# Zero fill in 10, 8 and 6 pieces, expert 0's W2 after the second gathers, and the last expert's first four tiles between its up passes

## The chip, the cores and the metric

One core of one Trainium2 chip. The metric is the device time of one execution in microseconds (us). A profile of one execution comes with each kernel; its times are us from the start of the span, and its engines are PE (TensorE), DVE (VectorE), ACT (ScalarE), POOL (GpSimd) and SP (SyncE). POOLq and SPq are the instruction queues of POOL and SP.

## The reference

Two layers in a row. First, chunked attention (4 batches, 8 heads, 768 tokens, head size 64): each chunk of 32 queries sees 16 tokens to the left, 8 to the right, and 8 memory tokens. Then a mixture of experts over the 3072 rows of 512 that come out.

```python
for c in range(nc):
    scores = scale * q_c @ concat([mem_k, k_ctx]).T
    out[:, :, c_start:c_end] = softmax(scores) @ concat([mem_v, v_ctx])
x = out.transpose(0, 2, 1, 3).reshape(3072, 512)
noisy_logits = x @ w_gate + log1p(exp(x @ w_noise)) * noise      # 8 experts
top2_w = softmax of the two largest noisy logits of each row
for e in range(8):
    out[mask] += top2_w[mask, k, None] * (relu(x[mask] @ w1[e]) @ w2[e])   # 512 -> 1024 -> 512
```

## The kernel before

**Attention and routing.** A loop runs over 16 pairs of heads, four pairs to a batch. When a batch `b` is finished, its rows stand in the SBUF tile `xrow`. They are written to a DRAM table `x_rows` in two parts by `put_rows`: the 256 words of the row itself, and behind them 8 words with the row's gates. `route(b)` picks the two experts of each row and counts out, expert by expert, a slot for it. Its steps are called by name: `s1`, `s1b` and `s2` make and compare the noisy logits, `s4` writes the gates, `s6` and `s7` add the batch's rows to the table of slots. `decode` turns that table into row numbers: `idx_s` after batch 1, `idx_a` after batch 2, `idx_f` after batch 3.

**Experts.** A slot table has 7 tiles for each expert: 6 of 128 rows and one of 64. Work is cut into ten sets of tiles, in this order: the first four ("sealed") tiles of experts 0 and 1, their last three tiles, and then all seven tiles of experts 2 to 7. For a set, `gather` (L633) fetches the rows of a tile from `x_rows` by an indirect DMA of POOL, `turn` (L656) transposes them on PE, `up` (L685) multiplies by W1 with a relu behind it, and `down` (L701, and L707 for the tile of 64) multiplies by W2. DVE or ACT scales the result by the gates into a tile `ys` (L710, L712), and POOL adds `ys` to the output by an indirect DMA (L713, the scatter). The scatters of the first set write instead of adding. A set's first scatter waits until all scatters of the set before have landed.

**Early start.** Experts 0 and 1 begin before routing is complete. Tiles 0 and 1 of both are gathered with `idx_s` (the first gathers, in `begin_first`), tiles 2 and 3 with `idx_a` (the second gathers), which need the rows and gates of batch 2 in `x_rows`; all others with `idx_f`, which need those of batch 3 too. On PE the order is: up for the first halves of sets 0 and 1, up for their second halves, down of set 0, up of set 2, down of set 1, and so on.

**Order by hand.** The program is scheduled by hand: what stands first in the code goes first into each engine's queue. POOL's queue holds, in this order, the first gathers, the load of W2 of expert 0 (`load_w2`, L585), the write of batch 3's rows, the second gathers, six gathers with `idx_f`, W2 of expert 1, four more gathers, and the first scatters with W1 of expert 2 (`load_w1`, L580) between them. SP's queue holds the zero fill of the output (`zero_fill`, L605) in three parts of 8 pieces (a piece is 128 rows of 2 KB) and the writes of gates (L346) between them. The first part of the fill is started by a small write to the zero tile on DVE (L893), so that it goes out at that place of DVE's queue and not at the start of the kernel.

**The last set.** `up_all` makes the up pass of the four sealed tiles (512 columns), with the turns of the other three between, and then the pass of the last three (320 columns). A `drain` on POOL (L799) and the seven tiles of `down` follow. The end of the kernel waits for the landing of the last scatter. A loop for rows that overflow the slots stands behind it and is not entered with these inputs.

Of the kernel before, what the change touches and what calls it, by code (L numbers as in the profile page):

```python
# [24 lines left out]
def kernel(  # L25
# [63 lines left out]
    def body():  # L89
# [493 lines left out]
        def load_w2(e):  # L583
            w2t = w2p.tile([128, FB, Dm], BF16, name="w2t")
            nc.gpsimd.dma_start(out=w2t, in_=moe_w2[e].rearrange("(fb p) d -> p fb d", p=128))  # L585
            W2[e] = w2t
# [85 lines left out]
        def up(s, c0=0, c1=None):  # L672
            e, tiles = sets[s]
            c1 = total(s) if c1 is None else c1
            if s not in hts:
                small = len(tiles) < NT
                hts[s] = (mp if small else pools["full"]).tile([128, FB, SEALED * CAP if small else SLOTS], BF16, name="hts" if small else "htf", bufs=2)
            k = -(-(c1 - c0) // 512)
            for f in range(FB):
                for c in range(k):  # L680
                    h = hring[cnt["h"] % 3] if hring else tr()
                    cnt["h"] += 1
                    lo, hi = c0 + c * (c1 - c0) // k, c0 + (c + 1) * (c1 - c0) // k
                    for kp in range(KP):
                        nc.tensor.matmul(out=h[:, :hi - lo], lhsT=W1[e][:, kp, f * 128:(f + 1) * 128], rhs=xTs[s][:, kp, lo:hi],  # L685
                                         start=(kp == 0), stop=(kp == KP - 1))
                    relu(hts[s][:, f, lo:hi], h[:, :hi - lo])
                yield "up", s, f

        def down(s, between=()):  # L690
            e, tiles = sets[s]
            ht = hts[s]
            for n, j in enumerate(tiles):
                y = yring[cnt["y"] % 2]
                cnt["y"] += 1
                o, w = (j - tiles[0]) * CAP, width(j)
                gate = gts[s][:, j:j + 1]
                ys = pools["full"].tile([128, Dm], F32, name="ys", bufs=NYS)
                if w == CAP:
                    for f in range(FB):  # L700
                        nc.tensor.matmul(out=y, lhsT=ht[:, f, o:o + w], rhs=W2[e][:, f, :], start=(f == 0), stop=(f == FB - 1))  # L701
                    wide, rows, idx = Dm, out_part[j], (idx_a if s < EARLY else idx_f)[:, e * NT + j:e * NT + j + 1]
                else:
                    wide, rows, idx = Dm // 2, out_part[j].rearrange("n (h d) -> (n h) d", h=2), idx_h[:, e:e + 1]
                    for f in range(FB):
                        for hh in range(2):
                            nc.tensor.matmul(out=y[64 * hh:64 * hh + 64, :wide], lhsT=ht[:, f, o:o + w], rhs=W2[e][:, f, hh * wide:(hh + 1) * wide],  # L707
                                             start=(f == 0), stop=(f == FB - 1))
                if on_act(j % 2):
                    nc.scalar.activation(out=ys[:, :wide], in_=y[:, :wide], func=Act.Copy, scale=gate)  # L710
                else:
                    nc.vector.tensor_scalar(out=ys[:, :wide], in0=y[:, :wide], scalar1=gate, scalar2=None, op0=Alu.mult)  # L712
                ins = nc.gpsimd.indirect_dma_start(  # L713
                    out=rows, out_offset=bass.IndirectOffsetOnAxis(ap=idx, axis=0), in_=ys[:, :wide], in_offset=None,
                    bounds_check=rows.shape[0] - 1, oob_is_err=True, **({"compute_op": Alu.add} if s else {}))

                if n == 0:
                    for old in scat.get(s - 1, ()):
                        tc.add_manual_dep(ins.ins, old.ins.name, mybir.DependencyInfo(mybir.DependencyClass.Sync, mybir.DependencyReason.DATA), reason="rows added to")
                scat.setdefault(s, []).append(ins)  # L720
                if n == 0:
                    for fn in between:
                        fn()
                for _ in range(-(-len(todo) // (len(tiles) - n))):
                    turn(*todo.pop(0))
                yield "down", s, j

        def every():
            half = FIRST * CAP

            def part(s, lo):
                def turns(s):
                    for j in range(lo // CAP, (lo + half) // CAP):
                        if (s, j) in got:
                            turn(s, j)

                turns(s)
                for at in up(s, lo, lo + half):
                    if at[2] == FB - 3 and s + 1 < EARLY:
                        turns(s + 1)  # L740
                    yield at

            for lo in (0, half):
                for s in range(EARLY):
                    yield from part(s, lo)
            def load(fn, e):
                return (lambda: fn(e),) if e < E else ()

            def up_all(s):
                if len(sets[s][1]) < NT:  # L750
                    yield from up(s)
                    return
                late = [(s, j) for j in range(SEALED, NT)]
                for at in up(s, 0, SEALED * CAP):
                    if late and at[2] % 2:
                        turn(*late.pop(0))
                    yield at
                yield from up(s, SEALED * CAP)

            yield from down(0, load(load_w1, EARLY))  # L760
            gather(2 * EARLY, ALL, idx_f, load(load_w2, EARLY))
            todo.extend((EARLY + 1, j) for j in sets[EARLY + 1][1])
            yield from up_all(EARLY)
            yield from down(1)
            gather(2 * EARLY + 1, ALL, idx_f, load(load_w1, EARLY + 1))

            order = [(t, j) for t in range(2 * EARLY + 2, NS) for j in range(NT)]
            runs = {}
            for d, k in zip(range(EARLY, NS - 2), (NT, NT, SEALED, SEALED, SEALED - 1, NT - SEALED)):
                runs[d], order = order[:k], order[k:]  # L770
            assert not order

            def run(d):
                for n, (t, j) in enumerate(runs[d]):
                    gather(t, (j,), idx_f)
                    if n == min(FIRST, len(runs[d]) - 1) and sets[d][0] + 3 < E:
                        load_w2(sets[d][0] + 3)

            for s in range(EARLY + 1, NS):
                e = sets[s][0]  # L780
                while todo and todo[0][0] <= s:
                    turn(*todo.pop(0))
                yield from up_all(s)
                if s < NS - 2:
                    ahead = [(s + 1, j) for j in sets[s + 1][1][:SEALED]]
                    if s < NS - 3:
                        todo.extend(ahead)
                    yield from down(s - 1, load(load_w1, e + 3))
                    run(s - 1)
                if s == NS - 3:  # L790
                    todo.extend(ahead)
                    yield from down(s)
                    run(s)
                if s == NS - 2:
                    todo.extend((s + 1, j) for j in sets[s + 1][1][:SEALED])
                    turn(*todo.pop(0))
                    turn(*todo.pop(0))
                    yield from down(s)
            nc.gpsimd.drain()  # L799
            yield from down(NS - 1)  # L800

        moe = every()

# [10 lines left out]
        def begin_first():  # L814
            decode(tabs[(B - 3) % 2][:, :EARLY * NT], idx_s, None)
            for s in range(EARLY):
                gather(s, range(FIRST), idx_s, upto=(B - 2) * S)
            load_w2(0)

        nc.gpsimd.memset(zt, 0.0)  # L820
        turn_pe(0, 0)
# [66 lines left out]
        warm(2)  # L888
        PV_pe(n - 1)
        exp_act(n)  # L890
        do(r, "s1b", "s2")

        nc.vector.memset(zt[:, :E], 0.0)  # L893
        zero_fill(0, 8)
        PT_pe(n)
        PT_copy(n)
        logits_pe(n - 3)
# [7 lines left out]
        logits_pe(n - 2)  # L905
        xT_pe(n - 1)
        mult_dve(n)
        put_rows(nc.gpsimd, B - 1, 0, XC)
        pctx.close()
        psE = ctx.enter_context(tc.psum_pool(name="psE", bufs=1, reuse_waits="tile"))  # L910
        bankE = [psE.tile([128, 512], F32, name=f"bankE{i}") for i in range(4)]
# [4 lines left out]
        xT_pe(n)  # L916
        do(r, "s4")
        put_rows(nc.sync, B - 2, XC, ROW)
        zero_fill(8, 8)
        do(r, "s5b")  # L920
        logits_pe(n - 1)
        units(1)
# [8 lines left out]
        decode(tabs[(B - 2) % 2][:, :EARLY * NT], idx_a, None)  # L931
        for s in range(EARLY):
            gather(s, range(FIRST, SEALED), idx_a, upto=(B - 1) * S)
        do(last, "s2")
        units(5)
        do(last, "s2b", "s3", "s2c", "s2d", "s4b", "s5", "s5c", "s4")
        put_rows(nc.sync, B - 1, XC, ROW)
        zero_fill(16, 8)
        do(last, "s5b")
        units(6)  # L940
        warm(4)
# [139 lines left out]
```

## Time and profile before

| | us |
|---|---|
| median of 3 runs (lowest, highest) | 331.51 (327.8, 333.48) |
| the profiled execution | 326.7 |
| its span, first to last instruction | 325.0 |

| engine | busy us | share of the span |
|---|---|---|
| PE matmul | 273.6 | 84% |
| POOL | 225.6 | 69% |
| DVE | 160.8 | 49% |
| ACT | 148.3 | 46% |

The span lies 1.7 us under the execution's own time. A share of busy time is a mean over stages: the first 120 us are attention and routing, the rest is the experts. The DMA queue of POOL is q0, that of SP is q1; both are served by the same 16 DMA engines. A row of the timeline gives start, duration, engine, line, operation, and in brackets the engine's idle time before it with what ended it. A row of the chain of waits gives start, duration and what the end of the kernel was then waiting for.

### The profile page before, as it was taken

The page shows a single profiled execution, that of the slowest core. Times are in us where ns is not written, and L with a number is a line of the kernel's source. Part 1 is how long each engine was busy: PE and PEld are TensorE (multiplying, and loading weights), DVE is VectorE, ACT ScalarE, POOL GpSimd, SP SyncE. Part 2 cuts the span into 40 slices and gives each one's busy share as a digit, 9 for nine tenths or more (in the row PEclk, how much of TensorE's full clock was granted, in tenths as well). Part 3 has the DMA queues.
Part 4 walks back from the last instruction along what each step waited for, and adds up shares of the span by engine and source line. Part 5 has one row for each costly group of instructions (what it writes and reads, how often), then busy time and mean ns, then how long its engine had stood idle before and what let it go on. Part 6 is the DMA issues. An engine that isn't in the chain of part 4 may idle for free.

```text
span 325.0 us, 7669 instructions
## 1 busy us (share of the span) xinstructions
PE 273.6 (84%) x3077; PEld 173.6 (53%) x3097; DVE 160.8 (49%) x367; ACT 148.3 (46%) x293; POOL 225.6 (69%) x219
## 2 busy tenths in 40 slices
PE   2878768787849719999999999999999999999940
PEld 1666656666638518565555465465454555555420
DVE  6478689889995823332344342342342434324210
ACT  6868878788656514224343423423422224234110
POOL 8997788667422178665888777887886888584480
PEclk9989989797998958999999999999999999999995
DMA  9999999999999996999999999999999979788393
GB/s 105 167 153 180 174 172 185 206 162 226 222 233 304 361 372 130 216 230 193 143 209 157 246 177 215 205 184 191 201 209 216 172 128 182 156 109 116 39 131 46
DMA packets 99847, 60.30 MB, mean 186 GB/s; under 512 B 65056, under 2 KB 84768, under 8 KB 99808
## 3 DMA queue, kind: packets, MB, share of 16 engines
q0 software_dynamic: 82160, 50.63, 107.0%
q1 hardware_dynamic: 14272, 8.98, 9.4%
q10 hardware_dynamic: 3376, 0.16, 1.0%
q8 instruction: 26, 0.43, 0.5%
q14 instruction: 13, 0.11, 0.1%
HBM read 65.07 MB, written 23.27 MB: 272 GB/s over the span
## 4 chain that ended last, share of the span: by engine, by line
PE 60%; DMA 10%; POOL 8%; issue 7%; DVE 7%; ACT 3%; POOLq 1%; DVEq 0%
PE bankE L701 22%; PE bankE L685 15%; PE bankT L685 8%; POOL out_dram L713 4%; PE bankT L656 4%; DMA x_rows<-xrow 3%; DMA xl<-x_rows,idx_s 3%; PE bankE L707 2%; DMA xl<-x_rows,idx_a 2%; DMA qg<-in_q_dram 2%; PE bankO L331 2%; PE bankT L257 2%; PE bankO L328 2%; POOL vp L134 1%; DVE mx L298 1%
## 5 line engine op out<-in xcount | busy, mean ns | idle before, releaser
L713 POOL DMA_INDIRECT out_dram<-ys,idx_f x40 | 62.9, 1574 | 24.1 <-DVE ys L712 12.7
L685 PEld LDWEIGHTS <-w1t 128*128 128x128 bf16 x576 | 55.3, 99 | 34.2 <-issue 3.9
L701 PE MATMUL bankE<-w2t,htf 128*128 128x512 bf16 x278 | 64.7, 379 | 0.5
L633 POOL DMA_INDIRECT xl<-x_rows,idx_f x48 | 50.0, 1042 | 16.2 <-issue 9.1
L712 DVE TENSOR_SCALAR ys<-bankE,gt 128x512 f32<-128x512 f32 (+1 forms) x32 | 21.9, 684 | 62.6 <-PE bankE L701 49.5
L685 PE MATMUL bankE<-xTf,w1t 128*128 128x320 bf16 (+1 forms) x250 | 51.3, 338 | 1.7 <-ACT xTf L658 1.3
L710 ACT ACTIVATE ys<-bankE,gt 128x512 f32<-128x512 f32 x24 | 16.5, 687 | 67.7 <-PE bankE L701 54.9
L701 PEld LDWEIGHTS <-htf 128*128 128x128 bf16 x288 | 27.4, 98 | 29.8 <-issue 0.2
L134 POOL DMA_DIRECT2D vp<-in_v_dram x34 | 33.6, 992 | 10.8 <-PE bankT L316 3.9
L670 DVE TENSOR_SCALAR htf<-bankE 128x512 bf16<-128x512 f32 (+1 forms) x32 | 18.9, 591 | 28.4 <-PE bankE L685 28.4
L668 ACT ACTIVATE htf<-bankE 128x512 bf16<-128x512 f32 (+1 forms) x32 | 16.5, 517 | 27.5 <-PE bankE L685 26.7
L685 PE MATMUL bankT<-xTf,w1t 128*128 128x320 bf16 (+1 forms) x128 | 27.8, 339 | 0.3 <-DVE htf L670 0.3
L267 ACT COPY kT<-bankT 64x768 bf16<-64x768 bf16 x32 | 25.3, 790 | 5.4 <-PE bankT L257 4.9
L656 PE MATMUL bankT<-identb,xl 128*128 128x128 bf16 (+1 forms) x224 | 20.7, 220 | 7.8 <-DMA xl<-x_rows,idx_a 5.7
L656 PEld LDWEIGHTS <-xl 128*128 128x128 bf16 (+1 forms) x224 | 15.5, 99 | 21.0 <-DMA xl<-x_rows,idx_a 6.7
L701 PE MATMUL bankE<-w2t,hts 128*128 128x512 bf16 x92 | 22.2, 379 | 0.2
L685 PE MATMUL bankE<-xTs,w1t 128*128 128x256 bf16 (+1 forms) x128 | 19.3, 291 | 0.7 <-ACT xTs L658 0.7
L298 DVE TENSOR_REDUCE mx<-bankS 128x12 f32<-128x768 f32 x16 | 15.2, 953 | 8.1 <-PE bankS L293 8.1
L257 PE MATMUL bankT<-identb,qg 128*64 128x128 bf16 x192 | 10.2, 253 | 10.2 <-DMA qg<-in_q_dram 8.1
L670 DVE TENSOR_SCALAR htf<-bankT 128x512 bf16<-128x512 f32 (+1 forms) x16 | 9.5, 591 | 15.6 <-PE bankT L685 14.4
L309 ACT ACTIVATE P<-sd 128x768 bf16<-128x768 f32 x16 | 13.5, 844 | 6.0 <-DVE sd L304 5.9
L713 POOL DMA_INDIRECT out_dram<-ys,idx_a x8 | 10.4, 1297 | 8.2 <-issue 4.2
(188 smaller groups left out, 451.3 us busy)
## 6 DMA issues: line engine op xcount, KB each, us to landing
w1t<-in_moe_w_dram POOLq DMA_DIRECT2D x8, 1024.0 KB, 12.3
w2t<-in_moe_w_dram POOLq DMA_DIRECT2D x8, 1024.0 KB, 10.7
out_dram<-zt SPq DMA_DIRECT2D x3, 2048.0 KB, 17.8
vp<-in_v_dram POOLq DMA_DIRECT2D x30, 168.0 KB, 8.2
qg<-in_q_dram POOLq DMA_DIRECT2D x16, 192.0 KB, 7.1
kg<-in_k_dram POOLq DMA_DIRECT2D x16, 192.0 KB, 7.4
x_rows<-xrow SPq DMA_DIRECT2D x2, 792.0 KB, 10.3
x_rows<-xrow SPq DMA_DIRECT2D x1, 768.0 KB, 8.5
```

What stands on the lines that cost most here:

```text
L134: nc.gpsimd.dma_start(out=vp[p0 + j:p0 + j + nj, c:c + m, hh, :], in_=bass.AP(v.tensor, v.offset + (hd * S + c * chunk + j - left_ctx) * D ...
L257: nc.tensor.transpose(out=p_t[64 * hh:64 * hh + 64, j, :], in_=src[:, hh, j * D:(j + 1) * D], identity=identb)
L267: nc.scalar.copy(kbufs[n % 2][hs, hh].rearrange("d (p j) -> d p j", j=SJ), p_t[hs])
L298: nc.vector.tensor_reduce(out=mx, in_=st[n]["ps"], axis=AX, op=Alu.max)
L633: nc.gpsimd.indirect_dma_start(out=xl, out_offset=None, in_=xd[:upto], in_offset=bass.IndirectOffsetOnAxis(ap=idx[:, c:c + 1], axis=0), bo ...
L656: nc.tensor.transpose(out=p_t[:, kp, :w], in_=xl[:w, kp * 64:(kp + 1) * 64].bitcast(BF16), identity=identb[:w, :w])
L668: nc.scalar.activation(out=dst, in_=src, func=Act.Relu)
L670: nc.vector.tensor_scalar(out=dst, in0=src, scalar1=0.0, scalar2=None, op0=Alu.max)
L685: nc.tensor.matmul(out=h[:, :hi - lo], lhsT=W1[e][:, kp, f * 128:(f + 1) * 128], rhs=xTs[s][:, kp, lo:hi], start=(kp == 0), stop=(kp == KP ...
L701: nc.tensor.matmul(out=y, lhsT=ht[:, f, o:o + w], rhs=W2[e][:, f, :], start=(f == 0), stop=(f == FB - 1))
L712: nc.vector.tensor_scalar(out=ys[:, :wide], in0=y[:, :wide], scalar1=gate, scalar2=None, op0=Alu.mult)
L713: ins = nc.gpsimd.indirect_dma_start(out=rows, out_offset=bass.IndirectOffsetOnAxis(ap=idx, axis=0), in_=ys[:, :wide], in_offset=None, bou ...
```

## The change

Five edits:

- The first part of the zero fill goes out ahead of routing steps `s1b` and `s2` of batch 2 on DVE, not behind them, and has 10 pieces. The second and third parts have 8 and 6.
- The write of batch 3's rows (768 KB) moves from POOL's queue to SP's, behind the gates of batch 2 and ahead of the second part of the fill.
- W2 of expert 0 is loaded behind the second gathers and no longer behind the first.
- In the last set, the down tiles 0 to 3 and their scatters stand between the two up passes, with the `drain` ahead of them; tiles 4 to 6 stay at the end.
- `down` gets an argument `of`, the tiles that it makes; the wait for the scatters of the set before is tied to the set's first tile.

```diff
-        def down(s, between=()):
+        def down(s, between=(), of=None):
...
-            for n, j in enumerate(tiles):
+            of = of or tiles
+            for n, j in enumerate(of):
...
-                if n == 0:
+                if j == tiles[0]:
                     for old in scat.get(s - 1, ()):
...
-            def up_all(s):
+            def up_all(s, middle=()):
...
                     yield at
+                yield from middle
                 yield from up(s, SEALED * CAP)
+
+            def sealed_down(s):
+                nc.gpsimd.drain()
+                yield from down(s, of=sets[s][1][:SEALED])
...
-                yield from up_all(s)
+                yield from up_all(s, sealed_down(s) if s == NS - 1 else ())
...
-            nc.gpsimd.drain()
-            yield from down(NS - 1)
+            yield from down(NS - 1, of=sets[NS - 1][1][SEALED:])
...
                 gather(s, range(FIRST), idx_s, upto=(B - 2) * S)
-            load_w2(0)
...
         exp_act(n)
+
+        nc.vector.memset(zt[:, :E], 0.0)
+        zero_fill(0, 10)
         do(r, "s1b", "s2")
-
-        nc.vector.memset(zt[:, :E], 0.0)
-        zero_fill(0, 8)
...
         mult_dve(n)
-        put_rows(nc.gpsimd, B - 1, 0, XC)
...
         put_rows(nc.sync, B - 2, XC, ROW)
-        zero_fill(8, 8)
+        put_rows(nc.sync, B - 1, 0, XC)
+        zero_fill(10, 8)
...
             gather(s, range(FIRST, SEALED), idx_a, upto=(B - 1) * S)
+        load_w2(0)
...
         put_rows(nc.sync, B - 1, XC, ROW)
-        zero_fill(16, 8)
+        zero_fill(18, 6)
```

More of the change, by code (lines that the diff above doesn't have):

```diff
@@ L723, in down @@
                         fn()
-                for _ in range(-(-len(todo) // (len(tiles) - n))):
+                for _ in range(-(-len(todo) // (len(of) - n))):
                     turn(*todo.pop(0))
```

## The prediction

> **What bounds the kernel now.** I read the page first, then the chain of waits from 80 to 125 us, PE's waits from 119 us on, POOL's timeline, and the chain at the end.
>
> ```profile
> span 325.0 us, 7669 instructions
> w2t<-in_moe_w_dram POOLq DMA_DIRECT2D x8, 1024.0 KB, 10.7
> out_dram<-zt SPq DMA_DIRECT2D x3, 2048.0 KB, 17.8
> ```
>
> The last two rows are DMA issues with the median time to landing: a W2 load takes 10.7 us, one part of the zero fill 17.8.
>
> ```profile
> 87.20 9.95 DMA xl<-x_rows,idx_s
> 97.20 0.61 PE bankT L656 x4
> ...
> 101.38 10.11 DMA x_rows<-xrow
> ...
> 112.30 0.33 POOL xl L633
> ...
> 113.88 6.64 DMA xl<-x_rows,idx_a
> 120.57 0.62 PE bankT L656 x4
> ```
>
> This is the chain where the stages meet. From 101.38 to 111.49 the kernel waits for 24 KB of batch 2's gates; they stand on SP's queue behind 2 MB of zeros. Only then can POOL issue the second gathers (112.30), and PE waits for these until 119.69.
>
> ```profile
> PE bankT L656 <- DMA xl<-x_rows,idx_a: 5.7, 2, 5.4
> PE bankE L685 <- ACT xTf L658: 1.3, 2, 0.7
> PE bankE L685 <- ACT xTs L658: 0.7, 1, 0.7
> PE bankT L685 <- DVE htf L670: 0.3, 1, 0.3
> ```
>
> From 119 us to the end PE waited for nothing but this: after the gathers 2.3 us in all. By this view alone PE is the bound, and every us that it starts earlier would be won. POOL's timeline says otherwise:
>
> ```profile
> 112.30 1.27 POOL L633 DMA_INDIRECT xl<-x_rows,idx_a  x1 [10.17 <-DVE xrow L438]
> ...
> 117.86 1.01 POOL L633 DMA_INDIRECT xl<-x_rows,idx_f  x1 [0.30 <-issue]
> ...
> 125.44 0.96 POOL L585 DMA_DIRECT2D w2t<-in_moe_w_dram  x1
> 126.70 1.09 POOL L633 DMA_INDIRECT xl<-x_rows,idx_f  x1 [0.30 <-issue]
> ...
> 133.39 1.04 POOL L713 DMA_INDIRECT out_dram<-ys,idx_a  x1 [1.65 <-DVE ys L712]
> ...
> 139.33 0.98 POOL L713 DMA_INDIRECT out_dram<-ys,idx_a  x1 [1.03 <-ACT ys L710]
> ...
> 148.97 1.63 POOL L713 DMA_INDIRECT out_dram<-ys,idx_a  x1 [3.63 <-issue]
> ...
> 283.91 1.62 POOL L713 DMA_INDIRECT out_dram<-ys,idx_f  x1 [2.70 <-DVE ys L712]
> ```
>
> Only the first set's scatters (133.39 to 139.33) start when their ys is done. The second set's first one goes at 148.97 and waits for the landing of the one issued at 139.33. The next view has the landing times of such scatters and, for a late set, the ys that its first scatter carries:
>
> ```profile
> out_dram<-ys,idx_a POOLq DMA_INDIRECT x5, 8.3
> ...
> 278.69 0.75 DVE L712 TENSOR_SCALAR ys<-bankE,gt 128x512 f32<-128x512 f32 x1 [1.35 <-PE bankE L701]
> ```
>
> 139.33 + 8.3 = 147.6, so the landing explains 148.97. At 283.91 the ys had been ready since 279.44, 4.5 us earlier, though the row names DVE as the last releaser: again the set before has to land. So from 133 us on two chains run side by side, PE with its matmuls, and POOL with scatters, gathers, loads and landings, and POOL's is the later one until the last set:
>
> ```profile
> 296.71 6.05 issue
> 302.76 0.03 POOLq L713
> ...
> 303.11 0.75 DVE L712 TENSOR_SCALAR ys<-bankE,gt 128x512 f32<-128x512 f32 x1 [1.24 <-PE bankE L701]
> 304.13 1.55 POOL L713 DMA_INDIRECT out_dram<-ys,idx_f  x1 [7.42 <-DVE ys L712]
> ...
> 315.28 1.55 POOL L713 DMA_INDIRECT out_dram<-ys,idx_h  x1 [0.30 <-issue]
> ```
>
> POOL's last scatter of the set before ends at 296.71, its queue goes on at 302.76 (the drain stands between), and PE's first ys is ready at 303.86. The two chains arrive 1 us apart, and seven scatters follow, (315.28 - 304.13)/6 = 1.86 us apart.
>
> **The change part by part.**
>
> *First part of the fill.*
>
> ```profile
> 91.77 0.20 DVE L386 TENSOR_TENSOR nl<-ns,nz_all 128x48 f32<-128x48 f32 x1
> ...
> 93.41 0.07 DVE L893 MEMSET zt<- 128x8 f32 x1
> 93.54 0.38 SPq L605 DMA_DIRECT2D out_dram<-zt  x1
> ...
> q1 hardware_dynamic: 379, 0.78, 56.8%
> q0 software_dynamic: 373, 0.38, 55.8%
> ...
> 112.00:117.00 5.00, 1.06 (x13) 0.89 (x13) 2.75 (x10) 0.00 (x0) 3.79 (x4) 0.70 1.07 376
> ```
>
> The small write goes ahead of s1b, which begins at 91.77: the fill is issued 93.41 - 91.77 = 1.6 us earlier. The two q rows are the DMA queues from 98 to 102 us, with packets and MB: SP's and POOL's share the engines packet for packet, and the fill moves at 0.78/4 = 195 GB/s. What stands in POOL's queue there is W2 of expert 0, and later the write of batch 3's rows. Both leave that queue. The last row (112 to 117 us, 376 GB/s at its end) is nearly the fill alone. So 10 pieces (2.62 MB) take 2.62/0.376 = 7.0 us instead of 2.1 MB in most of 17.8. With the first packets some 3.5 us after the issue, they are through by about 103 us and the gates of batch 2, written at 101.38, land by 105, not at 111.49. The two added pieces cost 0.52/0.376 = 1.4 us of that. The price is the first gathers, which land at 97.2 and now share engines with the fill for up to 97.2 - 95.5 = 1.7 us; packet for packet that is between 0 and 1.7 us. I take **+0.5**, since few of their packets are then left. It shifts all that follows on DVE.
>
> *Second gathers, PE.* They now wait for their row numbers:
>
> ```profile
> 105.74 0.17 DVE L570 TENSOR_TENSOR idx_a<-row,emp 128x14 int32<-128x14 f32 x1
> ...
> 115.55 0.22 DVE L570 TENSOR_TENSOR idx_f<-row,emp 128x56 int32<-128x56 f32 x1
> ...
> 112.64 0.90 PE L480 MATMUL bankT<-col,Rn 128*128 128x56 f16 x12 [1.20 <-DVE Rn L468]
> ```
>
> So they go at about 106.4 instead of 112.30. With 6.6 to 7.4 us to the turn, as before, PE can turn at about 113.9, just after the routing matmuls that end at 113.54, not at 119.69. PE leads by 5.8 us and avoids most of the slow clock after its wait (about 1 more).
>
> *W2 of expert 0.* POOL issues it behind four second gathers, 106.4 + 5.2 = 111.6. It shares engines with the second and third fill parts. Packet for packet with the rest of the third part I get the landing near 125 us; bounds are 111.6 + 10.7 = 122.3 (the page's median) and 111.6 + 17.8 = 129.4 (if it goes at the fill's pace). PE wants it for the down of set 0, at 130.86 before and about 124 now, so PE's lead shrinks to some 5 us. By the Trainium skill (DMA: Bandwidth & Descriptors, "Measured"), a lone 1 MB load is busy for 6.15 us; an estimate from that page would be a landing at 118 and no wait. No row here shows a weight load that fast; the sum would stay the same.
>
> *POOL's chain.* The gathers with idx_f wait for that table, 115.77 + 0.5, so they start at 116.3 instead of 117.86: **-1.5** us. The gates and rows of batch 3 must have landed too: SP now carries 2.62 + 0.79 + 2.1 = 5.5 MB ahead of these gates, at 300 to 376 GB/s from 95.5 on, 110 to 114. Six gathers, W2 of expert 1 and four gathers follow in 133.39 - 1.35 - 117.86 = 14.2 us (1.65 us of idle time, of which 0.3 stays), and then the first scatter, whose ys is ready (PE leads): 130.5, **-2.85**. One new wait: in this program POOL's DMAs take eight semaphores in turn, and the first gather behind W2 of expert 1 is the eighth DMA behind W2 of expert 0. It needs that landing (125) when it is due at 126.70 - 1.5 = 125.2; I add **+0.45**, between 0 and 129.4 - 125.2 = 4.2, near the end that my landing is nearest to. Queued behind it are three gathers and all scatters. So the chain is **-2.4** us. From 133 us on the rest of it is scatters, loads and landings that move as one, and I carry -2.4 to the drain. DMA agrees with a gain of that size and no more:
>
> ```profile
> 122.00:127.00 5.00, 5.00 (x41) 4.07 (x40) 1.60 (x4) 1.97 (x7) 4.09 (x5) 0.78 0.48 139
> ```
>
> From 122 to 127 us the DMA engines are half idle (0.48), some 2.6 us, and that gap is where W2 goes.
>
> *Last set.* PE does the same work in another order, and its relus are done before the down that needs them. The seven scatters now wait for POOL alone: 302.76 + 0.37 of queue + 0.26 = 303.4 instead of 304.13, **-0.75**. The last three can follow at 1.86 us: their ys come at or before. If PE had been late, the change would save here; with a lead of 5 us PE would have been early anyway. Bounds: 0 (1.86 us apart is POOL's own pace) and 302.76 - 304.13 = -1.4.
>
> **Sum:** -2.4 - 0.75 = **-3.15** us. Against the profiled execution 326.7 - 3.2 = 323.5; that execution lies 4.8 under the median, so for the runs I say 331.51 - 3.2 = **328.3**.
>
> **The rivals.**
>
> 1. *PE's lead goes through* (the gaps in POOL's chain are slack that shrinks). For it: PE's waits above. Gain 5.2 + 0.75 = 6, up to 5.8 + 1 + 0.75 = 7.6 if W2 is no wait: 323.9 to 325.5. Against it: scatters that start 4.5 us after their ys and wait for landings.
> 2. *W2 of expert 0 comes too late* (the other side). If its 1024 KB go at the shared 0.38/4 = 95 GB/s from 111.6 + 5 on, they need 11 us and land at 127.7, with slower engines 129.4. The gather that waits for its semaphore then goes at 129.4 instead of 126.70, the first scatter at 129.4 + 5.34 = 134.7 instead of 133.39, +1.35, less 0.75: +0.6, 332.1. It decides from a landing at 128 on.
> 3. *The larger fill keeps its old pace.* 17.8 x 1.25 = 22.2 us from 92 on: gates at 114, second gathers at 114.8, W2 issued at 120, landing at 130.7 by 10.7. The first scatter goes at 136.0, +2.6, and with loads pushed behind it up to +6: 334 to 337. Against it: what shared the engines with the fill is gone.
> 4. *Nothing moves*: the gates land early, but the gathers with idx_f do not, because batch 3's gates land at 118 behind more on SP's queue: -0.75 alone, 330.8.
>
> **How the numbers follow.** Forecast 0.46, rival 1 0.19, rival 2 0.13, rival 3 0.12, rival 4 0.10. 2% (6.6 us) is about what a measurement of this kernel can tell from no change; its own runs spread over 5.7 us. Faster by more than that is rival 1's upper half and a little of the forecast: 0.16. Slower is the upper end of rival 3 and loads pushed back in rival 2: 0.12. The range takes in rival 1 up to 7.6 us with 1 us of the runs' spread, and rivals 2 and 4 and the lower half of 3: 322.5 to 334.5.
>
> **What would show it.** Right: the second gathers issued near 106.4, PE turning at 114, the first fill landing some 7 us earlier; the gathers with idx_f near 116.3; the first scatter near 130.9, the second set's first one near 146.5, lags between ys and scatter 2 to 3 us larger than before, the sealed scatters right behind the drain at 300.3 to 301, the last one near 312.1. Wrong: the first scatter after 133.4, a PE wait for W2 of expert 0 beyond 2 us, or a drain that ends over 5 us earlier (rival 1).

## The result, and the profile after

The changed kernel takes 325.56 us (median of 20 runs, 323.05 to 328.23) where the kernel before takes 329.47 (20 runs, 325.81 to 333.48). The ratio is 0.9929, 95% interval 0.9903 to 0.9955: 0.7% faster, which is the same at the bound of 2%. Forecast was 328.3 us and a gain of 3.15 us; the medians differ by 3.9, the ratio is worth 2.3 us. Ratios leave out runs over 1.5% longer than the shortest of their kernel, which leaves only three or four runs in e7, e8, e9 and e12 below, so these have the medians of all runs beside them. The profiled execution took 325.68 us, against 326.7 before, so the two profiles differ by only 1.0 us; the section on the prediction comes back to that.

In these profiles the scatter's line is L714 and that of ys L711 or L713 (one or two lines further down in e7 to e11). Span and DMA issues of the changed kernel's page, as in the first fences of the prediction:

```profile
span 324.0 us, 7669 instructions
out_dram<-zt SPq DMA_DIRECT2D x1, 2560.0 KB, 9.6
```

The first part of the fill is now 2.5 MB and lands in 9.6 us, where a part of 2 MB took 17.8. Its issue and POOL's timeline:

```profile
94.53 0.38 SPq L605 DMA_DIRECT2D out_dram<-zt  x1
...
106.63 1.12 POOL L633 DMA_INDIRECT xl<-x_rows,idx_a  x1 [4.99 <-DVE idx_a L570]
...
112.34 0.99 POOL L585 DMA_DIRECT2D w2t<-in_moe_w_dram  x1
118.87 1.09 POOL L633 DMA_INDIRECT xl<-x_rows,idx_f  x1 [5.54 <-DVE hts L670]
...
126.54 0.96 POOL L585 DMA_DIRECT2D w2t<-in_moe_w_dram  x1
127.90 1.09 POOL L633 DMA_INDIRECT xl<-x_rows,idx_f  x1 [0.40 <-PE bankE L685]
...
133.26 1.04 POOL L714 DMA_INDIRECT out_dram<-ys,idx_a  x1 [0.30 <-issue]
...
148.52 1.63 POOL L714 DMA_INDIRECT out_dram<-ys,idx_a  x1 [3.27 <-DMA out_dram<-ys,idx_a]
...
284.00 1.62 POOL L714 DMA_INDIRECT out_dram<-ys,idx_f  x1 [2.69 <-DMA out_dram<-ys,idx_h]
...
303.93 1.55 POOL L714 DMA_INDIRECT out_dram<-ys,idx_f  x1 [7.11 <-DVE htf L670]
...
315.08 1.55 POOL L714 DMA_INDIRECT out_dram<-ys,idx_h  x1 [0.30 <-issue]
```

Set these beside the rows of before. The fill did not go out earlier in this execution (94.53, before 93.54): it landed early chiefly because W2 has left POOL's queue, as e3 shows below; what batch 3's rows add to that was not tested apart. The second gathers go at 106.63 and no longer at 112.30. But the gathers with `idx_f` start at 118.87, one us *later* than before (117.86), the first scatter at 133.26 (133.39), and the last at 315.08 (315.28). POOL's chain has not moved. PE's has:

```profile
114.72 0.71 PE L656 MATMUL bankT<-identb,xl 128*128 128x128 bf16 x8
...
277.21 0.75 DVE L713 TENSOR_SCALAR ys<-bankE,gt 128x512 f32<-128x512 f32 x1 [1.35 <-PE bankE L702]
```

PE turns the second gathers at 114.72 and not at 119.69. The ys of the scatter at 284.00 is ready at 277.96, 6.0 us ahead of it; before, it was 4.5 us ahead of the one at 283.91. So PE got a lead, and it stands in POOL's queue. But it is not the 5.0 us of the turn: the first ys on DVE is done at 129.85 and not at 133.11, 3.3 us earlier, and the one at 277.96 is 1.5 us earlier than its counterpart before (279.44). The gap in DMA between 122 and 127 us (0.48 busy before) is closed (windows: PE, PEld, DVE, ACT and POOL busy, granted clock, DMA share, GB/s):

```profile
122.00:127.00 5.00, 3.00 (x22) 1.82 (x19) 0.85 (x2) 0.90 (x3) 4.09 (x5) 1.00 1.06 265
```

Why did the start of POOL's chain not move? The row at 118.87 names DVE as its releaser, but the table was ready earlier:

```profile
115.86 0.22 DVE L570 TENSOR_TENSOR idx_f<-row,emp 128x56 int32<-128x56 f32 x1
```

It ends at 116.08, 0.2 us ahead of the forecast's 116.27 (115.77 + 0.5). The gathers wait another 2.8 us for the gates of batch 3, which SP issued at 112.31:

```profile
112.31 0.36 SPq L346 DMA_DIRECT2D x_rows<-xrow  x1
112.72 0.54 SPq L605 DMA_DIRECT2D out_dram<-zt  x1
```

In the trace the semaphore of a write is counted up in 16 steps. For this write 15 of them come between 114.48 and 116.14, the last at 118.09, and the gathers start 0.78 us behind it. The 0.78 us return in e3, e4 and e8 (119.55 and 120.33; 121.83 and 122.61; 118.49 and 119.27), so the gates' landing is what ended the wait. The fill ahead of the gates has a late step too (the trace has four of its 16, three at 111.79 to 111.83 and one at 114.62), which suggests that one share of the gates stood behind a share of the fill; that is not shown.

### The profile page after: what moved, and what is told of

The parts are those of the page before. It is cut to its first block, busy times and chain, and to the rows that moved or that the text cites. A ratio compares the mean times of both kernels' runs of the same rounds, so it can differ in the third digit from the quotient of the medians.

```text
span 324.0 us, 7669 instructions
## 1 busy us (share of the span) xinstructions
PE 276.9 (85%) x3077; PEld 175.0 (54%) x3097; DVE 161.6 (50%) x367; ACT 148.4 (46%) x293; POOL 225.4 (70%) x218
## 5 line engine op out<-in xcount | busy, mean ns | idle before, releaser
L714 POOL DMA_INDIRECT out_dram<-ys,idx_f x40 | 63.0, 1575 | 23.6 <-issue 8.2
L685 PEld LDWEIGHTS <-w1t 128*128 128x128 bf16 x576 | 54.5, 98 | 38.4 <-issue 7.3
L713 DVE TENSOR_SCALAR ys<-bankE,gt 128x512 f32<-128x512 f32 (+1 forms) x32 | 21.9, 684 | 61.4 <-PE bankE L702 41.4
L711 ACT ACTIVATE ys<-bankE,gt 128x512 f32<-128x512 f32 x24 | 16.5, 688 | 68.8 <-PE bankE L702 45.1
L670 DVE TENSOR_SCALAR htf<-bankE 128x512 bf16<-128x512 f32 (+1 forms) x32 | 18.9, 592 | 28.5 <-PE bankE L685 21.4
L656 PE MATMUL bankT<-identb,xl 128*128 128x128 bf16 (+1 forms) x224 | 20.0, 215 | 0.4 <-ACT xt L356 0.4
L343 DVE TENSOR_TENSOR xrow<-bankO,rec 128x768 bf16<-128x768 f32 x16 | 15.3, 958 | 0.9 <-DMA x_rows<-xrow 0.4
```

The costliest lines, as they stand in the source:

```text
L656: nc.tensor.transpose(out=p_t[:, kp, :w], in_=xl[:w, kp * 64:(kp + 1) * 64].bitcast(BF16), identity=identb[:w, :w])
L670: nc.vector.tensor_scalar(out=dst, in0=src, scalar1=0.0, scalar2=None, op0=Alu.max)
L714: ins = nc.gpsimd.indirect_dma_start(out=rows, out_offset=bass.IndirectOffsetOnAxis(ap=idx, axis=0), in_=ys[:, :wide], in_offset=None, bou ...
```

## Experiments

The table puts the kernels together; each number is the start of an instruction in that kernel's profile. "Gate wait" is POOL's idle time in front of the gather behind W2 of expert 1; 0.30 is no wait. "Set 9 last" is the last scatter of the last but one set. Medians and ratios are those of the runs, against the kernel before on the same chip. A profiled execution of this table can lie up to 1.8 us from its kernel's median (e1: 326.94 and 325.14), so two rows tell of 1 or 2 us only where the waits in them say so.

| kernel | `idx_f` gathers | gate wait | first scatter | set 9 last | last scatter | median us | ratio (95%) |
|---|---|---|---|---|---|---|---|
| before | 117.86 | 0.30 | 133.39 | 295.16 | 315.28 | 327.8 to 329.5 | 1 |
| after | 118.87 | 0.40 | 133.26 | 295.26 | 315.08 | 325.56 | 0.9929 (0.9903 to 0.9955) |
| e1 start only | 116.87 | 1.89 | 132.71 | 293.83 | 316.96 | 325.14 | 0.9925 (0.9895 to 0.9955) |
| e2 last set only | 117.53 | 0.30 | 134.59 | 294.13 | 315.52 | 327.12 | 0.9981 (0.995 to 1.0012) |
| e3 W2 early | 120.33 | 0.30 | 134.52 | 295.72 | 316.40 | 326.37 | 0.9948 (0.9911 to 0.9985) |
| e4 gates on ACT | 122.61 | 0.30 | 136.89 | 300.12 | 320.15 | 328.70 | 1.0006 (0.9967 to 1.0046) |
| e5 fill 10, 4, 10 | 117.18 | 4.56 | 135.71 | 297.06 | 316.32 | 326.91 | 0.9958 (0.9923 to 0.9993) |
| e6 no second fill | 115.68 | 2.44 | 132.10 | 293.63 | 312.90 | 323.33 | 0.9866 (0.9809 to 0.9923) |
| e10 e5 and gov early | 116.44 | 5.23 | 135.63 | 296.80 | 316.00 | 326.00 | 0.9938 (0.9913 to 0.9963) |
| e12 after again | 117.55 | 2.37 | 133.88 | 296.37 | 315.89 | 325.53 | 0.9841 (0.9796 to 0.9886), by medians 0.993 |

### The two halves of the change: e1 and e2

e1 is the changed kernel with the last set as before; e2 is the kernel before with the last set's new order.

```diff
 e1:
-yield from up_all(s, sealed_down(s) if s == NS - 1 else ())
+yield from up_all(s)
...
+nc.gpsimd.drain()
-yield from down(NS - 1, of=sets[NS - 1][1][SEALED:])
+yield from down(NS - 1)
```

> The changed kernel with its last set as before: seven down tiles behind both up passes. Theory (two chains that arrive together at the last set, POOL's and PE's; the edits at the start give PE a lead of 3 us or more that POOL's chain doesn't have): PE's ys of the last set wait for the drain and no longer the other way round, so the ratio is 0.991 to 0.997, about that of the whole change, the first scatter of the last set stands right behind the drain, and the lag between ys and scatter in the sets before is 2 to 3 us larger than before. Rival (PE is the bound): PE's lead goes through, ratio 0.985 to 0.990, lags as before. Rival (all of the gain is at the last set): ratio 0.998 to 1.002.

> The kernel before with nothing but the last set's order changed: tiles 0 to 3 of its down between the two up passes. Theory (two chains): PE is taken out of the tie at the end by 7 us, the seven scatters stand right behind the drain, ratio 0.992 to 0.998; not additive with the edits at the start, which do the same to PE by another way. Rival (PE is the bound): PE's order changes and its sum does not, ratio 0.998 to 1.002. Lags in the sets before the last: as before in both.

Measured: e1 0.9925, e2 0.9981. What can be measured comes from the start; the interval of e2 takes in no change and reaches into both of its forecasts. In e1's profile the first scatter of the last set waits for PE, not for the drain as expected. PE had been held up at 253 us by a load named `gov`, which the section on e9 explains:

```profile
253.56 0.36 DVE L977 TENSOR_TENSOR gov<-gov,miss 128x192 f32<-128x192 f32 x1 [3.46 <-DMA gov<-x_rows]
...
305.81 1.55 POOL L714 DMA_INDIRECT out_dram<-ys,idx_f  x1 [10.44 <-DVE ys L713]
```

PE lost 2.7 us there, and the granted clock was 0.79 from 254 to 262 us, where it was 1.00 in the changed kernel's profile. So in one execution PE can lose its lead and be the later chain at the end (10.44 us of idle time, where 7.11 stood after the drain in the changed kernel). The medians of e1 and of the changed kernel are alike.

In e2's profile the first scatter of the last set goes 1.25 us earlier than before (302.88), but the fifth waits for PE, whose second up pass now stands in front of it:

```profile
311.81 1.55 POOL L714 DMA_INDIRECT out_dram<-ys,idx_f  x1 [1.80 <-DVE ys L713]
```

So the new order alone gives nothing at the last scatter (315.52, before 315.28). The changed kernel has no wait there, but its fifth ys is ready at 308.80 for a scatter at 311.36: 2.6 us ahead, not the 6 us of the first.

### W2 of expert 0 early again: e3

```diff
 gather(s, range(FIRST), idx_s, upto=(B - 2) * S)
+load_w2(0)
...
 gather(s, range(FIRST, SEALED), idx_a, upto=(B - 1) * S)
-load_w2(0)
```

> The changed kernel with W2 of expert 0 loaded behind the first gathers again. Theory: the first part of the fill shares the engines with it again, the gates of batch 2 land 2 to 4 us later than in the changed kernel and the second gathers with them; PE's lead shrinks by as much and is not missed at the end; POOL's chain starts when batch 3's gates are there and has no wait for W2 of expert 0 (the first gather behind W2 of expert 1). Ratio to before 0.990 to 0.999, within 1.5 us of the changed kernel. Rival (PE is the bound): 2 to 4 us slower than the changed kernel.

Measured: 0.9948. The second gathers go at 111.92 again, as the fill shares the engines with W2, and the `idx_f` gathers at 120.33, as batch 3's gates land later (119.55). The gate wait is 0.30, because W2 has long landed. The first scatter is at 134.52. The second gathers are 5.3 us later than in the changed kernel, where 2 to 4 were expected. Loading W2 later is what gives the second gathers their 5 us, and about 1.3 us at the first scatter in these profiles.

### Batch 3's gates on a queue of their own: e4

```diff
-put_rows(nc.sync, B - 1, XC, ROW)
+put_rows(nc.scalar, B - 1, XC, ROW)
```

> The changed kernel with batch 3's gates written from ACT's queue, not from SP's behind the second part of the fill. Theory (POOL's chain decides, and it starts when batch 3's gates have landed, 118.1 us in the changed kernel): the gathers with the last table start when their row numbers are ready, 116.4 instead of 118.9, the first scatter goes 0.7 to 2.5 us earlier (the lower end if the landing of W2 of expert 0 then holds the chain) and the end with it: ratio 0.984 to 0.991. Rival (PE is the bound, or another wait takes over at once): the same as the changed kernel, 0.992 to 0.994.

Measured: 1.0006, the other way. From the page's DMA part of 100 to 125 us, and POOL's timeline:

```profile
x_rows<-xrow ACTq DMA_DIRECT2D x1, 24.0 KB, 8.8
...
122.61 1.09 POOL L633 DMA_INDIRECT xl<-x_rows,idx_f  x1 [8.51 <-DVE hts L670]
...
136.89 1.04 POOL L714 DMA_INDIRECT out_dram<-ys,idx_a  x1 [0.30 <-DVE ys L713]
```

24 KB took 8.8 us to land, and the gathers waited 8.51 us. The edit does more than was meant: SP no longer stops for these gates, so it issues the third part of the fill right behind the second, at 104 us and not at 112.72. From 113 to 116 us SP's queue moved 440 packets, of the fill, and ACT's none; ACT's first packets move between 116.5 and 117 us, as the fill runs out, and 673 of its 784 from 117 to 118. By the Trainium skill (DMA: Bandwidth & Descriptors, "Queues, rings and completion order") an engine goes round its queues packet by packet; this trace does not show that for ACT's queue and SP's, and why ACT's packets started so late is not shown. The last step of the gates' semaphore came at 121.83. What the run does show: with the start of POOL's chain 3.6 us later (136.89 to 133.26), the last scatter is 5.1 us later and the whole gain is gone, though PE's work is the same.

### No second fill part: e6

```diff
-zero_fill(10, 8)
```

> The changed kernel with the second part of the zero fill (8 pieces, 2 MB) left out, so that those rows of the output are not cleared; nothing else differs. It makes the two conditions of the forecast true that failed: batch 3's gates have no fill ahead of them and should land by 113 instead of 118.1, and W2 of expert 0 should land near 122 to 124 instead of 127. Theory (the start of POOL's chain sets the end): the gathers with idx_f at 116.4 instead of 118.87, no idle time before the gather behind W2 of expert 1, first scatter at 130.5 to 131 instead of 133.26, second set's first one near 146, and every scatter down to the last one about 2.3 us earlier; ratio to the kernel before 0.986. Rival (PE's chain sets the end since the change): PE starts no earlier than in the changed kernel, so the last scatter stays at 315 and the ratio at 0.993.

Measured: 0.9866. The `idx_f` gathers at 115.68 are those of the forecast (116.3), as the table is then all that they wait for. But the gather behind W2 of expert 1 waited:

```profile
123.34 0.96 POOL L585 DMA_DIRECT2D w2t<-in_moe_w_dram  x1
126.75 1.09 POOL L633 DMA_INDIRECT xl<-x_rows,idx_f  x1 [2.44 <-ACT gt L645]
```

The releaser shown is not the cause. In the trace this gather waits for the semaphore that W2 of expert 0 holds. Where the landing of W2 is on record, the gather goes 0.8 us behind it: 126.6 and 127.37 in e1, 127.7 and 128.54 in e12, 129.6 and 130.36 in e5. In e2 and e3, where W2 is loaded early, it waits 0.30 us. Here W2 lands near 126. That is the forecast's new wait, 2.1 us beyond the usual 0.30, where it put 0.45. The first scatter at 132.10 is 1.2 us earlier than in the changed kernel, not 2.3, and the last, at 312.90, 2.2 us: the ratio came as forecast, but half of the gain arose behind the start. PE is 1.9 us earlier here too (first ys of the last set at 296.14 and not at 297.99), which the rival had left out. What speaks against PE setting the end is that this ys lay ready for 5.6 us before its scatter at 301.75.

### The fill in 10, 4 and 10 pieces: e5

```diff
-zero_fill(10, 8)
+zero_fill(10, 4)
...
-zero_fill(18, 6)
+zero_fill(14, 10)
```

> The changed kernel with the zero fill cut as 10, 4 and 10 pieces instead of 10, 8 and 6: half of the second part goes behind batch 3's gates. Theory (the start of POOL's chain sets the end, and it has two gates, the landing of batch 3's gates and that of W2 of expert 0): the gates land near 115.5 instead of 118.1, so the gathers with idx_f start near 116.8 instead of 118.87, but as much fill as before still shares the engines with W2, which lands at 127 to 128, and the gather behind W2 of expert 1 waits for it; first scatter 132.5 to 133.3 instead of 133.26, time 0 to 0.7 us shorter than the changed kernel, ratio to the kernel before 0.991 to 0.993. Rival (the gates alone set the start): the whole 2 us, first scatter at 131.2, ratio 0.987.

Measured: 0.9958. The gates are no wait now (117.18, 3.0 us behind W2's issue, as the table is ready), but W2 is:

```profile
130.36 1.09 POOL L633 DMA_INDIRECT xl<-x_rows,idx_f  x1 [4.56 <-ACT gt L645]
...
PE bankE L702 <- DMA w2t<-in_moe_w_dram: 3.1, 1, 3.1
```

The two gates are as expected; the size was not. W2 took 16.4 us and landed at 129.6, not at 127 to 128, and PE waited for it too (3.1 us). What the gates gained W2 lost, and the first scatter was 2.4 us later. Two rows of the changed kernel's DMA from 118 to 122 us show the price (queue, packets, MB, share of the 16 engines):

```profile
q0 software_dynamic: 370, 0.38, 58.0%
q1 hardware_dynamic: 351, 0.71, 52.6%
```

W2's packets write 1 KB and the fill's 2 KB, their numbers are nearly equal, and each takes its engine about as long: 4 us x 16 x 0.58/370 = 100 ns, and 96 ns. So, counted in the profile's packet time, 1 MB of W2 costs the engines what 2 MB of fill cost, and beside the fill it moves at 95 GB/s.

### Less work on PE, less on POOL: e7, e8, e9, e11

e7 leaves out half of the second matmul of the seventh set, e8 four of its seven scatters, e9 both.

```diff
 e7:
+nf = FB // 2 if s == EARLY + 4 else FB
-for f in range(FB):
+for f in range(nf):
...
 e8:
+if s != EARLY + 4 or n < 2 or n == len(of) - 1:
-ins = nc.gpsimd.indirect_dma_start(
+    ins = nc.gpsimd.indirect_dma_start(
...
```

> The changed kernel with half of the second matmul left out in one set (24 matmuls of 512 columns of the seventh set, six tiles), so the rows of that set are wrong; scatters, loads and landings are all kept. PE has 5 us less to do from 239 us on. Theory (POOL's chain sets the end, PE is 3 to 6 us early): the lags between ys and scatter grow by about 5 us from that set on and the last scatter stays near 315: ratio to the kernel before 0.993, the changed kernel's own. Rival (PE sets the end): 5 us shorter, ratio 0.978.

Measured: median 326.39 against 325.56 of the changed kernel (ratio 0.9867, interval 0.9788 to 0.9947, by medians 0.992; too wide to tell the two theories apart). The profiled execution, of 326.42 us, does tell: the first ys of the last set, and its first and last scatter.

```profile
293.51 0.75 DVE L714 TENSOR_SCALAR ys<-bankE,gt 128x512 f32<-128x512 f32 x1 [1.26 <-PE bankE L703]
...
305.16 1.55 POOL L715 DMA_INDIRECT out_dram<-ys,idx_f  x1 [6.65 <-issue]
...
316.30 1.55 POOL L715 DMA_INDIRECT out_dram<-ys,idx_h  x1 [0.31 <-issue]
```

In the changed kernel this ys was ready at 297.99, 5.9 us ahead of its scatter; here at 294.26, 10.9 us ahead. Five us of PE's work were taken away, and in this execution all of them went into waiting for POOL.

> The changed kernel with four of the seven scatters of the seventh set left out (third to sixth tile), so those rows lack that expert; all matmuls are kept. POOL's chain is 4 x 1.86 = 7.4 us shorter at 253 us. Theory of two chains with PE's lead small at the end: the next set's first scatter at 257.0 instead of 264.4, then PE becomes the later chain (ys of the last but one set ready at 278.0, last ys at 311.3), so the last scatter goes near 311.6 instead of 315.1: 3.5 us shorter, ratio 0.982, and waits for ys are back in front of the last scatters. Rival 1 (PE sets the end already): no change, 0.993. Rival 2 (POOL alone, PE far ahead): the whole 7.4 us, 0.970.

Measured: 0.9822, interval 0.9756 to 0.9888, and a median of 323.39 (by medians 0.983): the number that two chains gave (0.982), between the two rivals. The profiled executions of e8 and e9 took 328.02 and 327.38 us, well above the medians, so waits are read from them and no times. In e8's the waits for ys are back, as expected:

```profile
303.76 1.55 POOL L715 DMA_INDIRECT out_dram<-ys,idx_f  x1 [7.15 <-DVE ys L713]
...
314.56 1.55 POOL L715 DMA_INDIRECT out_dram<-ys,idx_f  x1 [3.67 <-DVE ys L713]
```

But PE is 5 us later in that execution than in the changed kernel's (first ys of the last set at 303.25 and not at 297.99), so these rows alone do not show what the missing scatters did.

> The changed kernel with both cuts together: half of the second matmul of the seventh set and four of its seven scatters left out. Theory of two chains: PE is 5 us earlier and POOL 7.4 us, so the sum is bound by POOL again with PE 1 to 4 us ahead: 6.5 to 7.4 us shorter than the changed kernel, ratio near 0.972, more than the two single cuts together (0 and 3.5). If the two cuts simply add, PE's cut would have had to show alone.

Measured: 0.9806 (0.9732 to 0.988), median 323.75 (by medians 0.984). This missed: it should have been 0.972. PE's waits and DVE's row say what came between:

```profile
PE bankE L703 <- DVE ys L714: 7.0, 1, 7.0
...
255.29 0.36 DVE L978 TENSOR_TENSOR gov<-gov,miss 128x192 f32<-128x192 f32 x1 [7.72 <-DMA gov<-x_rows]
```

`gov` is a load of all gates for the loop on overflowing rows, 96 KB in packets of 32 bytes on ACT's queue. Its first use stands in DVE's queue ahead of a ys, and PE cannot go on before that ys. In e8 PE lost 2.6 us to it, and in the changed kernel the same load holds DVE for 1.05 us:

```profile
gov<-x_rows ACTq DMA_DIRECT2D x1, 96.0 KB, 27.1
...
252.08 0.36 DVE L976 TENSOR_TENSOR gov<-gov,miss 128x192 f32<-128x192 f32 x1 [1.05 <-DMA gov<-x_rows]
```

So PE's lead can end here: DVE was ready for `gov` at 247.57 in e9 and had it at 255.29, 29 us after its issue. It is not so each time: in e7 `gov` was used at 248.06 without a wait, 21.4 us after its issue, so PE's 5 us could pass. e11 is e9 with this load issued earlier:

```diff
-until("down", NS - 5, NT - 1)
+until("down", 3, NT - 1)
 gov = lp.tile([128, NP, E], F32, name="gov")
 nc.scalar.dma_start(out=gov, ...)
```

> The two cuts together (half of the second matmul of the seventh set and four of its seven scatters left out) with the gov load issued some 50 us earlier. With the two cuts alone PE waited 7.0 us for a ys that stood on DVE behind gov's landing, and that ate what the cuts should have given. Theory: with that wait gone PE is 5 us earlier, POOL 7.4 us, POOL is the later chain and the last scatter goes 6.5 to 7.4 us earlier than in the changed kernel, near 308: ratio to the kernel before 0.970 to 0.975. Rival (something else held the two cuts back): ratio stays near 0.981 with a wait somewhere else.

Measured: 0.9649 (0.9618 to 0.968), median 316.24 and the last scatter at 307.97 (forecast near 308): 9.3 us under the changed kernel, of which 7.1 show in the profile. The ratio lies below the forecast's 0.970 to 0.975; where the rest comes from is not shown. The load took as long as ever (28.1 us), but nothing waits for it. The first scatter of the last set waits for nothing but the drain, the fifth waits 1.2 us for a ys:

```profile
295.62 1.55 POOL L716 DMA_INDIRECT out_dram<-ys,idx_f  x1 [6.55 <-issue]
...
304.25 1.55 POOL L716 DMA_INDIRECT out_dram<-ys,idx_f  x1 [1.51 <-DVE ys L714]
...
307.97 1.55 POOL L716 DMA_INDIRECT out_dram<-ys,idx_h  x1 [0.30 <-issue]
```

So work pays where it is taken from both chains, once the third one (`gov`) is out of the way: the intervals of e9 and e11 do not meet. From PE alone it paid nothing in the profile, from POOL alone 2.2 us by medians and 3.5 by ratios. No run has the early `gov` with one cut only, so what each cut is worth without that wait is not shown.

### A version that might be better: e10, beside e12

e10 has the fill of e5 and the early `gov`; e12 is the changed kernel itself, on the same chip.

> The fill as 10, 4 and 10 pieces, and the load of the gates for the overflow (gov, 3072 packets of 32 bytes on ACT's queue) issued behind the fourth set's down instead of the sixth's, so some 50 us earlier. In the changed kernel it took 27 us to land and its first use stands on DVE in front of a ys. Theory (POOL sets the end, PE leads): the wait of DVE for gov goes (1.1 us in the changed kernel's profile, 3.5 to 7.7 in some of the others), PE's lead grows by that, and the time is at most 0.7 us shorter than the fill order alone makes it, since only executions in which PE was the later chain gain. Rival (PE's waits set the end): 1 to 3 us shorter.

> The changed kernel as it is, on the same chip as the fill order and the gov load, to compare them with: ratio to the kernel before 0.993.

Measured: e10 0.9938, median 326.00; e12 median 325.53, which is 0.993 of the 327.81 before, as expected. In e10 no wait of PE for ys is left, but W2 of expert 0 holds POOL for 5.23 us and PE for 2.9. Beside e5 (326.91) the early `gov` is worth 0.9 us, between the two forecasts and within the runs' spread. No version here beats the changed kernel.

## Why the prediction was right, and where it was not

**The chains.** The main reading held: PE's waits make PE look like the bound, but its lead is lost in POOL's queue. PE was to turn at 113.9 and turned at 114.72. The lags between ys and scatter were to grow by 2 to 3 us and grew by 1.5 (4.5 to 6.0), since only 1.5 us of PE's 5.0 are left at 278 us. In e7's profile 5 us less of PE give no us at the end. Rival 1 falls with that, as far as one execution tells.

**The fill.** The second gathers were forecast for 106.4 and went at 106.63. Rival 3 falls: 2.5 MB landed in 9.6 us. The part of the reason that failed is the issue 1.6 us earlier: it came 1.0 us later. The price on DVE, +0.5, held in this profile (the table of the second gathers is ready at 106.37, before at 105.91), but it is 1.0 to 2.3 us in e1, e7, e9, e11 and e12; e2, with the old start, has 0.7, so part of it is the spread between executions.

**The start of POOL's chain, -1.5.** This step failed in the profile: +1.0. The table was in time, but the gates of batch 3 were taken to land between 110 and 114 and landed at 118.09. The forecast divided bytes by a rate. That misses when SP can issue (112.31, behind the routing) and the one late share. The time is that of rival 4, but its reason, more fill ahead on SP's queue, holds for one late share at most: that queue had all but run empty (10 packets from 112 to 113 us), and 15 of 16 shares had landed by 116.14. In e1, e7, e9, e11 and e12, which have the same order of transfers there, SP issued the gates at 112.9 to 114.2 and they had landed by 116.0 to 117.0, before the table. There the gathers went at 116.87 to 118.21, because the table itself was later: 1.0 us earlier than before at best, and 0.4 later at worst.

**The eight-semaphore wait, +0.45.** The mechanism was right and the size was wrong. Where the gates were in time, the wait was 1.6 to 4.9 us beyond the usual 0.30 (1.89 in e1, 2.37 in e12, 4.56 in e5, 5.23 in e10). W2 was taken to land at 125; it landed near 126 even with 2 MB less of fill (e6). In the changed kernel's profile the late gates hide it (0.40): POOL's chain has two gates that feed on the same DMA engines, and bytes moved from one to the other (e5) only change which is last. So -2.4 became -0.1 in that profile, and in all seven profiles with this order of transfers the first scatter goes between 132.71 and 134.38, where 130.9 was forecast. (The working also says that the sum would stay the same if W2 landed at 118 without a wait; by its own terms it would be -3.6.)

**The last set, -0.75.** POOL's chain reaches the last set 0.1 us later than before (295.26 and 295.16), and its first scatter goes 0.2 us earlier (303.93 and 304.13), so the term measured -0.3: the wait behind the set before shrank from 7.42 to 7.11 us, and 6.55 is seen where nothing else is late (e11). In e2 the runs cannot tell it from nothing, and the prediction's "the last three can follow at 1.86 us" failed there: the fifth scatter waited for PE.

**The sum.** The two profiles give -1.0 us (326.7 to 325.68), of which the last scatter's start has 0.2 and what comes behind it 0.8. The runs give -2.3 by the ratio. The range held and the number was near, but not by the path that was worked out, so the nearness is luck: the two terms that made it up, -2.4 and -0.75, measured -0.1 and -0.3. The signs set down for POOL's chain did not come true (second set 148.52 and not 146.5, sealed scatters from 303.93 and not from 300.3 to 301, the last one at 315.08 and not at 312.1). The forecast's level, 328.3, came from a median of 3 runs of before (331.51) that was 329.47 with 20.

What gives the runs their larger gain is not shown. The profiled execution of before is among its shortest (326.7, with medians of 327.8 to 329.5), that of the changed kernel is an ordinary one (325.68 to 325.56). A reading that fits: before, the two chains arrive 1 us apart, so an execution in which either one stumbles is longer; afterwards PE is 6 us ahead at the first scatter of the last set and 2.6 at the fifth, and smaller stumbles, such as the wait for `gov` (0 to 3.5 us in the profiles without a cut), cost nothing. e1 and e2 put the gain at the start, where PE gets that lead, and in e7's profile more lead gives no more. But no profile of a longer execution of before was taken, and in e1's profile PE had no lead left, so this is argued, not shown.

## What to carry to other kernels

Look for the second chain before you price a wait: compare when a result is ready with when it is used, set by set, and take from the earlier chain nothing but insurance against its own stumbles. Where several transfers of one stage share the same DMA engines, price the stage by all its packets together; here a change of order (e5) decided which consumer was last and did not shorten the stage. And do not take a small DMA for a quick one: 24 KB or 96 KB in 32-byte packets on a queue of their own were the latest thing in their stage (e4, e9).

## What was not expected of the hardware

- 24 KB in 768 packets took 8.8 us from issue to landing on ACT's queue (e4). None of them moved before 116.5 us, 3.4 us after the issue, while SP's queue moved the fill. 96 KB in 3072 packets took 24 to 29 us beside loads and scatters in the eleven profiles that have the landing, and at most 21.4 us in e7.
- One share of a write can be late: 15 of the 16 steps of the gates' semaphore came by 116.14 us, the last at 118.09, and the gathers waited for it.
- A load that converts f32 to bf16 costs per packet as much as a fill of twice the written bytes: 100 ns for 1 KB against 96 ns for 2 KB.
- The granted clock is 1.00 from 122 to 127 us in the changed kernel, where 0.78 was granted before, when PE had waited longer (in e1, too, 0.79 was granted for the 8 us behind a wait of 2.7 us); yet in that window PE was busy for 3.00 us of 5, and it lost two stretches without a shown cause:

```profile
125.16 0.60 PE L685 MATMUL bankE<-xTs,w1t 128*128 128x256 bf16 x4 [0.89 <-issue]
126.53 0.60 PE L685 MATMUL bankE<-xTs,w1t 128*128 128x256 bf16 x4 [0.78 <-issue]
```
